# Layer norm's variance scaling on ScalarE, decays loaded ahead in two pieces, and a new order of work

## The chip, the cores and the metric

One core of a Trainium2 chip. The metric is the device time of one execution, in microseconds. The engines are named as in the profile: PE (TensorE, the matmuls), PEld (its weight loads), DVE (VectorE), ACT (ScalarE), POOL (GpSimd) and SP (SyncE, which here issues every transfer).

## What is computed

The reference is a chain of three layers on a batch of 4 sequences of 768 tokens, all in float32: a linear attention with decaying state (8 heads of 48), a gated layer with a spatial product over tokens, and a second gate with a convolution over 5 tokens.

```python
# attention, per batch and head, token by token
cur = einsum('bhd,bhe->bhde', u[None] * kt, vt)
y[:, :, t] = einsum('bhd,bhde->bhe', rt, state + cur)
state = wt[:, :, :, None] * state + einsum('bhd,bhe->bhde', kt, vt)
# gated layer: 384 -> 2 x 512 -> 384
u, v = split(gelu(x @ w_in))
v_n = (v - mean(v)) / sqrt(var(v) + 1e-06) * g_ln
gated = u * (einsum('ts,bsd->btd', w_sg, v_n) + b_sg[None, :, None])
x = x + gated @ w_out
# second gate
gate = sigmoid(causal_conv5(x, conv_w))
out = (gate * (x @ w_val)) @ w_out2
```

## The kernel before

**Attention.** The 768 tokens of a batch are cut into 3 segments of 256, the 8 heads into 4 pairs, which gives 48 units (batch, segment, pair), numbered in that order. Each unit loads one packet (`load_unit`, word "pk"): 128 rows of 773 columns, of which the first 261 are the decays, then 256 of k and 256 of r. Two scans along the decays on DVE give the products of decays after (F, `suffix`) and before (E, `prefix`) each token in chunks of 64; both read the decays alone. POOL or DVE multiplies r by E (L) and k by F (K). PE transposes K (t), forms scores (s), the states' growth (B) and the output (C). ACT copies out of PSUM (kx, gx, yc, ox), DVE masks the scores (mx), adds up the states (a), carries them to the next segment (z) and adds to the output (yx). U is ACT's start of a segment's state from the carried one. In the first batch only, ACT also forms the current token's term (ow), and PE runs filler matmuls on constants ("wm", "wps"). From the third batch on POOL forms that term (`bonus`).

**The other layers.** Per batch the output is transposed on PE (xT, with ACT and DVE splitting it into a high and a low part, xTo). Then come the layer's second half with its layer norm (hv, ln), the first half (u), the product over tokens (vs, vso, gate), the first output product (wo, woo), the convolution (cv), the value product (val, valo) and the last product (out), whose three tiles of 128 tokens ACT copies and SP sends off (outo). Every product is done in three passes of high and low parts. The weights come as float64 and are decoded by one ACT and four DVE instructions each (`to_f32`, word "dec"), then split ("spl"); "wl" are their loads. The token weights are loaded by "sg", v by "nat" and "sv", the constants by "ld". The wl loads share buffers: wl6 to wl8 overwrite the buffer of wl3 and wl4, which dec3 and dec4 read.

**Layer norm** (`hv`, lines 687 to 699), for each of 24 token tiles: ACT applies gelu and sums (line 691), centres (692), squares and sums (693); DVE scales the sum of squares to the variance with eps (line 695, 128x1); POOL raises it to the power -1/2 (696); ACT and DVE write the high and the low part (697, 698).

**The order of work.** Each step records its instructions under a word, such as "ln0" for the first layer norm, instead of issuing them. `SCHEDULE` (lines 55 to 193) lists the words; each mention issues the next part of the word: up to 16 instructions in a row on PE, 3 for some words, otherwise one (lines 956 to 969). An instruction that uses another engine starts a new part. So the list fixes the order on every engine and on SP's queue of transfers, while what waits for what follows from the tiles:

```python
            for _ in range(int(times or 1)):
                for f, a, k in parts[word].pop(0):
                    f(*a, **k)
```

In the profile all these instructions have line 969, the loop that issues them, so they are told apart by tile. Packets of the units have the tiles pk, room_l or room_w; F and E are the scans' outputs; st are states; s and rsw are ACT's copies; vg, vnt, sm and rstd belong to the layer norm; ot is the output tile, p and o are PSUM.

Of the kernel before, what the change touches and what calls it, by code (L numbers as in the profile page):

```python
# [70 lines left out]
yc8 a6 ox9 s8 spl4 ow26 mx11 B7 spl8 yx8 a6 C6 ow25 sg4 F9 gx23 K9 gx21 z6 U9 wm35 a7 gx22 yd5 ow24  # L71
wm35 mx12 wm36 U8 a7 wm36 E9 ow27 ox10 t9 ox11 kx13 kx12 q9 L9 ow31 B8 yx10 ow30 ln0 yx9 ow29 a7 ln0
yc10 s9 F10 ow28 C7 spl8 nat3 sv11 kx14 yc9 ln0 sg3 yx11 xT2 E10 pk12 wm37 ln1 xTo2 wm37 wl9 wm38
gx26 xTo2 hv2 ox12 gx25 K10 gx24 mx13 ln1 z7 a8 wm38 yd6 a8 hv2 ow34 q10 yc11 ow35 a8 yd7 ow33 hv2
F11 U10 L10 ow32 C8 ln2 mx14 B9 ln0 s10 pk13 E11 xT3 t10 q11 wm39 L11 ox14 gx27 wm39 wm40 yc12 gx28
a9 wm40 kx15 K11 yc13 xTo3 yx12 mx15 a9 gx29 s11 q12 kx16 ox13 a9 C9 ow38 ln2 F12 U11 ln2 B10 spl7
K12 ow37 t11 spl7 ow36 wm41 yx13 kx17 xTo3 hv3 gx30 gx32 a10 gx31 yd8 spl6 wm41 wm42 a10 q13 ox15
wm42 ow39 spl6 ow43 mx16 B11 yx14 ln2 mx17 a10 C10 ow40 E12 ow42 yc14 hv3 gx34 F13 L12 ow41 gx33
ox17 hv3 gx35 yx16 ox16 yc15 a11 ow47 yd9 pk14 yx15 yc16 ln1 ow45 s12 ln3 t12 K13 a11 dec6 a11 C11
E13 kx18 wm43 ow44 ln2 L13 ow46 wm43 spl12 nat4 yx17 xT4 mx19 sv12 yc17 F14 yd10 kx19 t13 xTo4 pk15  # L80
s13 spl13 B12 spl12 yd11 ln3 xT5 mx18 dec8 ln3 xTo4 hv4 kx20 spl13 gx36 xTo5 hv4 dec8 ln3 E14 hv4
gx37 dec8 L14 dec9 xTo5 hv5 gx38 a12 ln4 dec8 hv5 dec9 dec8 hv5 a12 wl11 dec9 u0 F15 ld2 ox18 ln5
o12 u0 ln4 ln3 u1 ln4 u1 mx20 z12 K14 ln4 B13 q14 s14 K15 C12 dec9 u1 ln4 sv14 wl13 vs0 E15 dec11
t14 dec9 vs0 dec11 spl15 vs0 wl10 q15 uo1 pk16 dec11 spl15 gx40 sv13 vs2 yc18 kx21 ln5 dec11 wl12
ln5 gx41 vs0 yx18 vs0 dec11 L15 dec10 gx39 u0 dec10 mx21 spl16 dec10 vs2 a13 uo0 dec10 spl16 spl14
vs1 dec10 a13 ox19 F16 ln5 vs1 o13 dec13 vs1 cw0 z13 q16 dec12 vs2 dec13 ln5 vs2 dec12 vs1 dec13 vs2
dec12 dec13 vs1 dec12 vs2 dec13 vs1 dec12 spl18 spl14 s15 spl17 wl15 B14 K16 C13 i0 E16 t15 spl17
# [956 lines left out]
```

## Time and profile before

| | |
|---|---|
| median of 3 runs | 474.2 us (473.36 to 474.63) |
| the profiled execution | 474.3 us, of which the span of its instructions is 472.5 us |
| mean granted clock of PE | 0.992 |
| busy: PE, PEld, DVE, ACT, POOL | 450.6, 406.3, 385.0, 266.9, 162.3 us |
| moved by DMA | 48.91 MB |
| sizes of the first loads | packet 386.5 KB, a piece of w_in 512.0, v 384.0, sv 96.0, ident 64.0, misc 38.5 KB |
| chain that ended last | PE 77%, DVE 9%, ACT 5% |

Times in rows are microseconds from the start of the span, unless marked ns. A busy time is the union of the engine's instructions. A bracket behind a row holds the engine's idle time ahead of the instruction and what ended it. The clock is the share of full speed that PE was granted.

### The profile page before, as it was taken

What the parts mean: (1) busy time and instruction counts of PE and PEld (TensorE: products, weight loads), DVE (VectorE), ACT (ScalarE), POOL (GpSimd) and SP (SyncE); (2) the same over time, 40 slices, a digit from 0 to 9 for tenths busy, and PEclk for the clock granted to TensorE, in tenths of its full rate; (3) what the DMA queues carried; (4) which work ended last, traced back from release to release, by engine and by line L of the source; (5) the groups of instructions that cost most, each with busy time, mean ns of one, the idle gap of its engine ahead of it and who ended that gap; (6) DMA issues with size and microseconds to landing.
All of it is one profiled execution on the core that took longest, in us unless ns stands there. A gap on an engine that the chain in (4) does not pass through costs nothing.

```text
span 472.5 us, 13805 instructions
## 1 busy us (share of the span) xinstructions
PE 450.6 (95%) x5556; PEld 406.3 (86%) x5556; DVE 385.0 (81%) x944; ACT 266.9 (56%) x786; POOL 162.3 (34%) x221
## 2 busy tenths in 40 slices
...
GB/s 278 354 261 167 1 163 111 187 154 114 130 50 116 157 185 68 60 74 152 125 67 135 171 92 85 51 85 135 54 39 147 10 2 1 50 2 0 1 1 100
DMA packets 27088, 48.91 MB, mean 103 GB/s; under 512 B 3088, under 2 KB 17168, under 8 KB 27024
## 3 DMA queue, kind: packets, MB, share of 16 engines
...
q8 instruction: 43, 0.70, 0.6%
q14 instruction: 21, 0.17, 0.1%
...
## 4 chain that ended last, share of the span: by engine, by line
PE 77%; DVE 9%; ACT 5%; issue 1%; DMA 1%; SPq 0%; ACTq 0%; DVEq 0%
PE vps L969 19%; PE p L969 13%; PE hv L969 10%; PE c L969 9%; PE ups L969 9%; PE o L969 8%; PE val L969 7%; PE a L969 2%; DVE cvp L969 1%; DVE st L969 1%; ACT st L969 1%; ACT vg L969 1%; DVE y L969 1%; DVE F L969 1%; DVE vps L969 1%
## 5 line engine op out<-in xcount | busy, mean ns | idle before, releaser
L969 PE MATMUL vps<-wsg,vnt 128*128 128x384 f32 x576 | 115.5, 339 | 1.4 <-DVE gt L969 0.7
L969 PEld LDWEIGHTS vps<-wsg,vnt 128*128 128x128 f32 x576 | 100.3, 188 | 3.0 <-ACT ut L969 1.6
L969 PE MATMUL ups<-x,win 128*128 128x384 f32 x288 | 61.4, 340 | 0.8 <-DVE gl L969 0.8
L969 ACT ACTIVATE st<-p,F 128x48 f32<-128x48 f32 x144 | 40.3, 304 | 38.0 <-PE p L969 36.7
L969 POOL TENSOR_TENSOR L<-pk,E 128x256 f32<-128x256 f32 x38 | 28.3, 744 | 94.7 <-PE p L969 32.9
L969 PE MATMUL c<-gl,late 128*128 128x384 f32 x288 | 59.9, 339 | 0.0
L969 PE MATMUL hv<-win,x 128*128 128x512 f32 x216 | 59.3, 405 | 0.3 <-ACT x L969 0.3
L969 DVE SCALAR_TENSOR_TENSOR cvp<-x,cw_col,cvp 128x384 f32<-128x384 f32 x84 | 50.6, 613 | 2.1 <-ACT cvp L969 1.6
L969 PEld LDWEIGHTS ups<-x,win 128*128 128x128 f32 x288 | 50.6, 188 | 1.7 <-DVE gl L969 1.1
L969 PEld LDWEIGHTS c<-gl,late 128*128 128x128 f32 x288 | 50.2, 188 | 1.0
L969 DVE SCALAR_TENSOR_TENSOR st<-st,F 128x48 f32<-128x48 f32 x128 | 39.3, 307 | 14.0 <-ACT st L969 13.0
L969 PE MATMUL o<-late,ml 128*128 128x384 f32 x216 | 46.9, 343 | 0.2
L969 PEld LDWEIGHTS hv<-win,x 128*128 128x128 f32 x216 | 38.7, 188 | 8.3 <-DVE x L969 0.9
L969 PE MATMUL val<-x2hl,late 128*128 128x384 f32 x216 | 43.6, 340 | 0.8 <-ACT ut L969 0.8
L969 POOL TENSOR_TENSOR x<-x 128x384 f32<-128x384 f32 x24 | 25.4, 1070 | 44.7 <-DVE cvp L969 43.0
L969 PEld LDWEIGHTS o<-late,ml 128*128 128x128 f32 x216 | 37.9, 188 | 2.8 <-DVE ml L969 1.4
L969 PEld LDWEIGHTS val<-x2hl,late 128*128 128x128 f32 x216 | 37.5, 188 | 1.9 <-ACT ut L969 1.1
L969 ACT ACTIVATE gl<-vps 128x384 fp32r<-128x384 f32 x29 | 14.3, 493 | 33.8 <-DVE vps L969 20.1
L969 POOL TENSOR_TENSOR y<-s,y 128x96 f32<-128x96 f32 x48 | 22.2, 469 | 32.2 <-DVE y L969 17.1
L969 DVE TENSOR_TENSOR_SCAN F<-pk,D1F 128x260 f32<-128x260 f32 x40 | 28.9, 722 | 4.5 <-DMA pk<-in_pk_dram 4.3
L969 POOL TENSOR_TENSOR rstd<-rstd,misc 128x1 f32<-128x1 f32 x24 | 15.6, 650 | 46.0 <-DVE rstd L969 32.3
L969 ACT ACTIVATE ut<-ups 128x384 f32<-128x384 f32 x32 | 15.7, 490 | 25.5 <-PE ups L969 20.6
(133 smaller groups left out, 944.5 us busy)
## 6 DMA issues: line engine op xcount, KB each, us to landing
pk<-in_pk_dram SPq DMA_DIRECT2D x40, 386.5 KB, 3.5
v<-in_v_dram SPq DMA_DIRECT2D x12, 384.0 KB, 4.9
out_dram<-ot SPq DMA_DIRECT2D x24, 192.0 KB, 1.9
rk<-in_rk_dram SPq DMA_DIRECT2D x12, 384.0 KB, 3.3
sv<-in_sv_dram SPq DMA_DIRECT2D x39, 96.0 KB, 3.0
bits<-in_w_in_dram SPq DMA_DIRECT2D x6, 512.0 KB, 7.4
room_l<-in_pk_dram SPq DMA_DIRECT2D x7, 386.5 KB, 6.7
bits<-in_w_o_dram SPq DMA_DIRECT2D x7, 384.0 KB, 4.2
```

Of the source, the lines that this page charges most:

```text
L969: f(*a, **k)
```

## The change

The variance's scaling and eps move from a DVE instruction to an ACT one (Identity with scale and a bias tile, which POOL fills at the start). The packets of units 0 and 1 are each loaded by two transfers, the decays first. Of the very last output tile ACT copies 208 columns and DVE 176. The words "rk" and "bon" are named by batch, and the list of words is written anew throughout. Its beginning, the part around the first layer norms and the last line stand here, then the rest of the diff.

```diff
@@ -53,144 +53,146 @@
 SCHEDULE = """
-ini0 pk0 zp0 wps0 pk1 pk2 ld0 wl0 ld1 wl1 nat0 F0 wl2 E0 sv0 q0 L0 F1 wl4 K0 pk3 E1 s0 dec0 sv3 wm4
-F2 L1 wl3 wm4 wm0 dec0 t0 K1 q1 nat1 kx0 dec1 t1 dec0 kx1 s1 E2 sv9 B0 dec1 wm1 gx1 L2 mx1 gx2 wm2
-mx0 dec1 wm9 dec2 K2 sv10 wm9 dec1 wm10 pk4 gx0 ox0 kx2 B1 dec0 dec4 sv1 wm10 dec2 wm3 a0 dec2 t2 a0
-C0 sv2 dec2 sg0 s2 dec1 wm5 ox1 yc0 kx3 wm6 ow2 dec4 gx4 wm7 F3 ow0 sg1 wm8 kx4 gx5 wm11 ow6 K3 z0
-wm12 mx2 dec3 wm13 dec0 pk5 gx3 wm15 wl5 ow3 dec4 ox2 pk7 ow7 q2 B2 ow1 dec2 spl1 sv4 wm14 a1 spl0
-dec3 wm15 wm16 a1 dec3 wm16 E3 q3 L3 mx3 yx0 yx1 wm21 dec4 t3 dec3 s3 C1 dec4 wm17 gx7 dec3 wm18
-spl10 wm19 F4 yc1 wm20 wl6 ox3 ow5 yd0 wm23 ow9 sv6 spl9 wm21 spl10 K4 wm22 pk6 wm22 spl2 z1 wl7 mx4
-E4 yc2 wl8 ow4 U4 sv5 kx5 spl9 L4 gx6 sv7 B3 yx2 pk10 dec5 a2 wm24 sv8 gx8 q4 ow10 s4 sg2 a2 ow8 C2
...
-C4 dec7 spl5 xTo1 hv1 ox7 kx9 U6 mx10 ow18 F7 hv0 spl3 ow20 sg5 gx17 ox8 gx15 ow23 z4 mx8 yc6 kx10
-a5 ow16 wm31 K7 ow22 mx9 wm31 yx6 gx16 wm32 q6 ln0 wm32 a5 hv1 dec6 a5 wm33 E7 hv1 F8 spl4 L7 wm33
-wm34 ln1 t7 q7 C5 E8 B6 s7 dec7 L8 wm34 gx18 z5 gx20 a6 ow21 K8 kx11 yx7 ln1 gx19 q8 yc7 U7 t8 yd4
...
-valo23*2 out69 out68 outo21 out67 outo21 out70 out71 outo22*2 outo23*2"""
+ini0 pk0 zp1 wps0 pk1 pk0 wl0 pk2 ld1 F0 pk1 wl2 E0 ld0 K0 nat0 F1 wl1 L0 dec0 wl4 E1 dec0 wl3 wm4
+q0 sv0 s0 dec0 F2 wm0 pk3 K1 wm4 wm1 dec0 t0 L1 t1 kx0 sv1 dec2 E2 pk4 kx1 s1 wm2 q1 wl5 L2 dec2 B0
+K2 wm3 gx1 mx1 ox0 mx0 gx0 pk5 dec2 dec1 wm9 dec0 wm5 ow0 wm9 gx2 wm6 q2 wm10 dec1 dec4 sv8 wm10 a0
+dec1 wm7 kx2 dec2 s2 B1 a0 dec3 sv4 dec1 wm8 sv2 wm11 dec2 t2 wm12 dec1 spl2 wm13 dec4 C0 spl0 dec3
+ow2 F3 kx4 gx5 ox1 ox2 K3 mx2 ow5 gx3 z0 dec3 yc1 kx3 wm15 gx4 E3 wm14 wm15 q3 B2 L3 mx4 yx0 wm16
+dec4 pk10 wm16 a1 sg0 dec3 s3 sv5 a1 C1 sv9 dec3 nat1 wm17 dec4 spl9 sv6 wm18 F4 t3 ow3 sg1 gx7 sv3
+ow1 K4 mx3 ox3 kx5 z1 yx1 yc0 spl9 ow9 zp0 wm21 gx6 ow4 wm19 a2 gx8 dec4 B3 ow6 dec5 a2 wl6 wm21 E4
+ow11 wm22 ow8 pk6 wm22 q4 spl10 L4 sv7 C2 mx5 ow7 sg2 z2 F5 yd0 s4 pk9 wm20 wl7 dec5 K5 t4 wm23 sv11
+kx6 yx4 ox4 wm24 yc3 E5 sv10 kx7 wm25 gx9 yc2 pk8 ox5 ow10 dec5 L5 U4 mx6 gx10 yx2 gx11 pk7 dec5
...
+mx8 hv0 kx10 xTo1 ox8 kx9 gx15 F7 hv1 spl3 spl4 sg5 U5 pk11 hv1 mx10 ow21 mx9 nat2 ow17 a5 U6 hv1 K7
+gx16 sg3 z4 ow23 a5 ow19 wm31 gx17 q6 wm31 ln1 a5 C5 E7 B6 F8 L7 wm32*2 dec7 ox7 t7 U8 K8 ow20 s7 z5
+yx6 yx7 gx19 dec7 yc6 ox9 ow22 wm33 gx18 E8 ow27 wm33 hv0 kx11 q7 yc7 gx20 a6 wm34 yd4 U7 a6 ln0
...
+out65 valo22 out66 valo23*2 out69 out68 outo21 out71 outo21 out67 out70 outo22*2 outo23*3"""
@@ -233,6 +235,7 @@
     cw_col = const.tile([128, KD, TAPS], F32, name="cw_col")
     win = const.tile([128, 2, KD, 2 * DV], F32R, name="win")
     D1F = const.tile([128, NW + 1], F32, name="D1F")
+    eps_col = const.tile([128, 1], F32, name="eps_col")
     u_bc = const.tile([128, DM], F32, name="u_bc")
 
 
@@ -368,12 +371,12 @@
 
     def load_rk(i):
         t = buf("rk", i, i // KS).rearrange("p (two f) -> p two f", two=2)
-        with step("rk"):
+        with step(f"rkb{i // KS}x"):
             sp.dma_start(out=t, in_=rk_[i // KS, i % KS * 128:(i % KS + 1) * 128, :, :])
 
     def bonus(b, i):
         s, j = divmod(i, NT)
-        with step("bon"):
+        with step(f"bonb{b}x"):
             t = buf("rk", b * KS + i, b)
             q = t[:, 0:DM]
             pool.tensor_tensor(out=q, in0=q, in1=t[:, DM:2 * DM], op=ALU.mult)
@@ -390,7 +393,8 @@
     def load_unit(n):
         b, s, p = units[n]
         with step("pk"):
-            sp.dma_start(out=buf("pk", n), in_=pk[b, p, s])
+            for x, y in ((0, OK_), (OK_, PK)) if n < 2 else ((0, PK),):
+                sp.dma_start(out=buf("pk", n)[:, x:y], in_=pk[b, p, s, :, x:y])
 
     def load_sv(n):
         b, s, p = units[n]
@@ -692,7 +696,7 @@
             act.activation(out=vg, in_=vg, func=AF.Identity, scale=-float(DV), bias=sm[:, 0:1])
             act.activation(out=hi, in_=vg, func=AF.Square, accum_out=sm[:, 1:2])
             rs = r2.tile([128, 1], F32, tag="rstd", name="rstd")
-            dve.tensor_scalar(out=rs, in0=sm[:, 1:2], scalar1=1.0 / DV, scalar2=EPS * DV * DV, op0=ALU.mult, op1=ALU.add)
+            act.activation(out=rs, in_=sm[:, 1:2], func=AF.Identity, scale=1.0 / DV, bias=eps_col)
             pool.tensor_tensor(out=rs, in0=rs, in1=mhalf, op=ALU.pow)
             act.activation(out=hi, in_=vg, func=AF.Copy, scale=rs)
             dve.scalar_tensor_tensor(out=vnt[b][:, 1, i, :], in0=vg, scalar=rs, in1=hi.bitcast(F32),
@@ -836,7 +840,10 @@
             for j in range(3):
                 with step("outo"):
                     t = rgt.tile([128, DM], F32, tag="t", name="ot")
-                    act.activation(out=t, in_=acc2[0][j], func=AF.Copy, scale=0.5)
+                    cut = 208 if (b, hf, j) == (B - 1, 1, 2) else DM
+                    act.activation(out=t[:, 0:cut], in_=acc2[0][j][:, 0:cut], func=AF.Copy, scale=0.5)
+                    if cut < DM:
+                        dve.tensor_scalar_mul(out=t[:, cut:DM], in0=acc2[0][j][:, cut:DM], scalar1=0.5)
                     t0 = hf * HALF + j * 128
                     sp.dma_start(out=out[b, t0:t0 + 128, :], in_=t)
 
@@ -883,6 +890,8 @@
     with step("ini"):
         dve.memset(D1F, 0.0)
         dve.memset(D1F[:, 0:NW + 1:W1], 1.0)
+    with step("zp"):
+        pool.memset(eps_col, EPS * DV * DV)
     for t in every("D1E"):
         with step("zp"):
             pool.memset(t, 0.0)
```

## Rows read from the trace of the kernel before

**Rows 1.** Busy time by stage: stretch, length, PE, PEld, DVE, ACT, POOL, clock, DMA, GB/s.

```profile
0.00:11.00 11.00, 7.66 (x61) 3.67 (x61) 5.70 (x13) 2.13 (x3) 4.09 (x9) 1.00 0.80 268
11.00:45.00 34.00, 27.54 (x559) 21.81 (x558) 33.72 (x92) 22.81 (x87) 15.03 (x17) 1.00 0.79 275
45.00:61.00 16.00, 13.34 (x286) 10.36 (x283) 11.60 (x35) 12.72 (x45) 8.89 (x14) 0.79 0.15 43
61.00:93.00 32.00, 30.49 (x523) 24.51 (x520) 29.81 (x88) 27.69 (x98) 14.96 (x20) 1.00 0.47 145
93.00:133.00 40.00, 36.19 (x476) 33.11 (x477) 39.52 (x104) 22.82 (x67) 17.21 (x23) 1.00 0.41 130
...
160.00:463.00 303.00, 303.00 (x3122) 283.93 (x3121) 237.75 (x546) 162.29 (x435) 93.22 (x125) 1.00 0.24 74
```

**Rows 2.** DVE in order of time: start, duration, what, idle time before.

```profile
4.11 0.70 DVE L969 TENSOR_TENSOR_SCAN F<-pk,D1F 128x260 f32<-128x260 f32 x1 [2.83 <-DMA pk<-in_pk_dram]
...
10.47 0.43 DVE L969 TENSOR_SCALAR spare<-spare 128x512 f32<-128x512 f32 x1 [1.26 <-ACT spare L969]
...
35.21 0.70 DVE L969 TENSOR_TENSOR_SCAN F<-room_l,D1F 128x260 f32<-128x260 f32 x1
...
42.88 0.84 DVE L969 TENSOR_TENSOR_SCAN F<-room_w,D1F 128x260 f32<-128x260 f32 x1
...
51.28 0.27 DVE L969 SCALAR_TENSOR_TENSOR st<-st,F 128x48 f32<-128x48 f32 x1 [1.87 <-ACT st L969]
...
51.64 0.14 DVE L969 TENSOR_SCALAR rstd<-sm 128x1 f32<-128x1 f32 x1
51.70 0.42 DVE L969 TENSOR_TENSOR pk<-pk 128x256 f32<-128x256 f32 x1
...
55.66 0.27 DVE L969 SCALAR_TENSOR_TENSOR st<-st,F 128x48 f32<-128x48 f32 x1 [0.88 <-ACT st L969]
```

**Rows 3.** DMA: KB each, us to landing; at 0-3, 43-47, 25-42 us, whole run.

```profile
bits<-in_w_in_dram SPq DMA_DIRECT2D x1, 512.0 KB, 7.2
...
spare<-in_w_sgT_dram SPq DMA_DIRECT2D x2, 192.0 KB, 2.5
...
DMA packets 2206, 4.28 MB, mean 252 GB/s; under 512 B 232, under 2 KB 1158, under 8 KB 2202
...
out_dram<-ot SPq DMA_DIRECT2D x24, 192.0 KB, 1.9
```

**Rows 4.** ACT in order of time.

```profile
9.76 0.68 ACT L969 ACTIVATE spare<-bits 128x512 f32<-128x512 f32 x1 [7.74 <-DMA bits<-in_w_in_dram]
...
45.07 1.28 ACT L969 ACT_TABLE_LOAD   x1
...
50.97 0.47 ACT L969 ACTIVATE st<-p,F 128x48 f32<-128x48 f32 x2
...
469.22 0.49 ACT L969 ACTIVATE ot<-o 128x384 f32<-128x384 f32 x1 [0.42 <-DMA out_dram<-ot]
```

**Rows 5.** PE in order of time.

```profile
12.31 0.45 PE L969 MATMUL p<-v,kn 64*64 64x48 f32 x16 [1.29 <-DMA v<-in_v_dram]
...
52.29 0.47 PE L969 MATMUL p<-ident,kh 128*128 128x128 f32 x1 [1.42 <-ACT s L969]
...
465.63 3.11 PE L969 MATMUL o<-late,ml 128*128 128x384 f32 x15
```

**Rows 6.** Busy time by stage, columns as in rows 1, five microseconds alone.

```profile
55.00:60.00 5.00, 4.97 (x98) 3.79 (x94) 3.20 (x11) 3.34 (x18) 3.64 (x6) 0.61 0.11 22
```

**Rows 7.** Groups of instructions, DVE and ACT: count, busy us, mean ns, idle before.

```profile
L969 DVE TENSOR_SCALAR rstd<-sm 128x1 f32<-128x1 f32 x24 | 3.4, 145 | 2.0 <-ACT vnt L969 1.8
...
L969 ACT ACTIVATE y<-v,rsw 128x48 f32<-128x48 f32 x48 | 14.9, 345 | 0.1
```

**Rows 8.** SP's issues of transfers in order of time.

```profile
25.88 0.33 SPq L969 DMA_DIRECT2D bits<-in_w_o_dram  x1
...
26.73 0.71 SPq L969 DMA_DIRECT2D room_l<-in_pk_dram  x1
```

More of the change, by code (lines that the diff above doesn't have):

```diff
@@ L71 @@
[L71 to L87, printed above, removed]
@@ L98 @@
-u6 yx22 o17 gate4 pk21 yd16 cv1 sv17 gate4 uo6 a17 gate4 cv2 a17 val0 cv1 kx25 U19 val0 a17 cv0 val0
-z17 cv0 cv2 val1 cv1 mx25 xT7 valo0 t19 s19 F20 valo0 B18 C17 cv2 valo0 out0 gx54 sv19 yc23 kx26 a18
-cv2 gx55 out1 gx56 U20 a18 vs5 E20 vs5 cv2 L20 vs5 yx23 cv2 a18 yd17 valo1 ox24 out2 o18 mx26 z18
-K20 valo1 C18 q20 s20 F21 pk22 B19 sv20 t20 valo1 vs5 gx57 E21 gx58 kx27 vs5 xTo7 a19 L21 mx27 out4
-yx24 out3 a19 gx59 K21 ox25 yc24 out5 a19 U21 o19 z19 xTo7 s21 yd18 C19 q21 F22 B20 pk23 sv21 t21
@@ new lines @@
+kx12 wm35 a7 wm36 K9 ox11 spl6 mx12 wm36 yx10 a7 yc9 ln0 B8 E9 ow24 gx23 ow28 t9 a7 ow29 L9 yx9 C7
+F10 ow30 ow31 ln0 ln1 s9 nat3 gx24 pk12 spl8 a8 ln1 yx11 xT2 ld2 yc10 E10 gx25 wm37 xTo2 wm37 wm38
+q9 ox12 L10 kx14 wm38 xTo2 yc11 hv2 ow33 q10 yd6 gx26 ln1 a8 hv2 K10 mx13 ln0 z7 a8 hv2 yd7 F11 spl7
+spl8 C8 ln2 mx14 s10 q12 t10 B9 E11 wm39 pk13 ln0 U9 L11 wm39 gx28 wm40 wl9 gx27 mx16 xT3 ow35 a9
+wl8 kx16 wm40 gx29 K11 kx15 a9 ow32 B10 ox14 yc12 ow39 q11 s11 ox13 ln2 a9 C9 xTo3 F12 ln2 ow34 t11
@@ new lines @@
+U10 mx15 spl7 xTo3 hv3 ln2 yx13 yx12 ow38 E12 hv3 yc14 gx30 gx31 a10 ow37 wm41 dec6 gx32 wm41 wm42
+U11 a10 ow36 wm42 a10 yc13 ox15 K12 kx17 C10 yd8 ow40 F13 ow42 B11 L12 ow41 ow43 hv3 yc16 ln1 ox17
+gx34 yc15 spl6 ox16 pk14 ow45 gx35 yx14 gx33 ln3 mx17 yx15 a11 yd9 yx16 t12 a11 K13 s12 q13 wm43 a11
+ow47 E13 ow46 C11 ln3 ln2 ow44 L13 wm43 kx18 spl13 yx17 xT4 kx19 mx18 yc17 F14 yd10 spl12 pk15 B12
+xTo4 nat4 s13 spl12 yd11 sv12 t13 xTo4 dec8 hv4 ln3 mx19 gx37 spl13 ox18 gx36 xT5 kx20 hv4 E14 xTo5
@@ new lines @@
+vs5 uo4 K19 ox23 gate4 u6 a17 pk21 mx25 cv0 u6 q20 gate4 u6 a17 yx22 val0 uo6 a17 cv1 val0 woo2 vs5
+z17 val0 cv2 F20 yc22 U19 s19 yd16 cv2 B18 o17 valo0 t19 cv2 valo0 C17 K20 U20 valo0 out0 gx54 cv1
+cv2 yc23 val1 gx56 gx55 a18 cv2 ox24 val1 o18 mx26 out1 cv2 a18 kx26 E20 xT7 val1 a18 xTo7 L20 yx23
+out2 z18 valo1 t20 pk22 F21 valo1 s20 B19 valo1 C18 E21 out3 gx57 sv20 gx58 a19 kx27 sv19 vs5 a19
+gx59 K21 yc24 ox25 out5 U21 a19 o19 mx27 out4 z19 L21 yx24 q21 B20 yd18 xTo7 s21 yd17 C19 F22 t21
```

216 lines of the change are left out of this document (112 added, 104 removed).

## The prediction

> **What bounds the kernel now.** I read first the table of busy time by stage [rows 1]. From 160 to 463 us the matmul engine (PE) is never idle: 303.00 of 303.00 us, while VectorE (DVE) works 237.75 us and ScalarE (ACT) 162.29 us. No change can make that stretch shorter, only open gaps in it. So a gain has to come from the 160 us before it, or from the last ten. Before 133 us the engine with the least idle time is DVE: its busy times in the first five stages are 5.70, 33.72, 11.60, 29.81 and 39.52 us, together 120.35 of 133 us. Its idle time is 5.30 us in the first 11 us, 0.28 in the next 34, 4.40 from 45 to 61 us, 2.19 up to 93 and 0.48 up to 133: 12.65 us. PE runs filler matmuls ("wm") in that time and still has gaps. I take the first 133 us to be bound by DVE's list of work plus DVE's idle time, and the rest by PE. So the sum is made of what DVE's idle time loses or gains, and of DVE instructions that leave its list ahead of that point.
>
> Second I read what DVE waits for in the two stages with idle time: at the start the first packet and then, by way of ACT, the first piece of the input weights; from 45 to 61 us the state copies of ACT [rows 2].
>
> **The head: transfers in pieces, and their new order.** Before, DVE's first scan starts at 4.11 us after 2.83 us idle, when all 386.5 KB of the packet are there [rows 2]. Now it needs 261 of 773 columns, 130.5 KB. A transfer of 192 KB on a quiet queue takes 2.5 us from issue to landing [rows 3]; I take 2.4 us, so the scan starts at 3.1 us, 1.0 us sooner (ends: 1.2 us, and nothing if the pieces issued behind it compete fully). But the next wait takes some of this back. DVE's list is now F0, E0, F1, E1 and then the decode step dec0 of the weights, ahead of q0 and F2, which stood ahead of it before. The four scans with their reciprocals are about 3.4 us, so DVE is free at 6.5 us. ACT can start dec0 when the first piece of w_in has landed; that was at 9.76 us [rows 4], with 1710 KB queued up to its end. Now 130.5 + 130.5 + 256 + 512 = 1029 KB are, and it is issued half a microsecond sooner. In proportion to the bytes still queued that gives 6.6 us; with the 7.2 us that it took from issue to landing [rows 3] it is 9.3 us. I take 7.2 us, near the first, since the shorter queue is what differs. With 0.7 us of ACT the decode starts on DVE at 7.9 us, after 1.4 us idle. DVE's idle time in the head is then 0.9 + 1.8 + 1.5 = 4.2 us against 5.30, a lead of 1.1 us (1.7 and -1.0 at the two ends). The two added issues on SP are covered: the queue is what limits, and v, for which PE waits 1.29 us at 12.31 us [rows 5], has 2670 KB up to its end in either order, so it lands as before. The second decode, dec1, has its weights 3182 KB deep instead of 2286 and may cost DVE up to 0.7 us. I book **-0.8 us** for the head.
>
> **45 to 61 us: the new order on ACT.** ACT loads a table for 1.28 us at 45.07 us, then runs the three long layer norm activations of one token tile, a split of 0.5 us, and the three of the next tile; only at 50.97 us come the state copies [rows 4]. So a tile's three take some 2.1 us. For the copies DVE waits 1.87 us and, 4 us later, another 0.88 us [rows 2]. PE has a gap of 1.42 us there, behind ACT [rows 5], and after it the granted clock falls to 0.61 of full speed, a mix of 1.2 and 2.4 GHz [rows 6]. In the new order one tile's three activations (ln1) go first, then ox7, U8, ow20, gx19, yc6, ox9, ow22, gx18, ow27, kx11, yc7, gx20, U7, and the other tile's three (ln0) only behind them. The block ahead of the state copies is shorter by 2.1 us and the 0.5 us split, but seven short activations of some 0.24 us stand ahead of gx18, which DVE's a6 needs. Net the copies come some 0.9 us sooner, and so does yc7, the one that PE waited for. The second block then falls into the 3.3 us in which ACT is idle in this stage [rows 1]. Ends: nothing, if the wait turns up one unit later, and 3.5 us, if the clock stays up and both waits go. I take **-1.5 us**, between, since the waits are shortened and not removed.
>
> **The variance scaling.** 24 VectorE instructions of 128x1 go, of 145 ns each [rows 7]; the next instruction starts 0.06 us behind one of them [rows 2], so six in the DVE-bound stretch are worth 0.4 to 0.9 us, and I take **-0.4 us**, since the next start is what counts on a full engine. The other 18 lie where PE is full and save nothing. On ACT 24 instructions of 128x1 with pointer operands come in. The trace has none; the nearest are the 128x48 products with a pointer scale, 345 ns long [rows 7]. I take 0.2 us, since a part of each lies under the next (ends 0 and 0.3). ACT is idle 4.3 of the 32 us from 61 to 93 us [rows 1], and six at 0.2 us are 1.2 us; a third of it on the path is **+0.4 us** (0 to 1.8). GpSimd's power now waits for ACT instead of DVE; behind it on GpSimd stand splits and products of later units, and who waits for its result is ACT, much later. The Trainium skill's page "ScalarE: Activation LUTs", section "Rules for kernel authors", speaks against this edit: adds and multiplications belong on VectorE. Its section "What ACT_TABLE_LOAD costs" gives 280 ns for an activation with a pointer bias, 93 ns of it overlapped, an estimate of 0.19 us each. By that rule the edit loses, as in the third rival.
>
> **The rest of the order.** DVE's list ahead of the first output product (word out0) has 339 instructions before and 335 after: six scalings gone, K20 and q20 added. No work is moved out of the bound stretch, and I book 0; what it may open on SP is the second rival. The renamed words add nothing. The memset of eps goes to GpSimd, which is idle 6.9 of the first 11 us [rows 1], and costs nothing; were it late, the first activation with it would wait, at about 55 us.
>
> **The tail.** The last tile's copy is 0.49 us on ACT, from 469.22 us, after 0.42 us of waiting for the transfer that frees its buffer [rows 4]. With 208 columns on ACT and 176 on DVE it takes some 0.33 us. But the matmul group that now comes last is the middle tile's: its copy can start only after PE's end at 468.74 us [rows 5], half a microsecond later than before, ahead of the last tile's first part on ACT. The last part is done at 469.55 to 469.7 us instead of 469.71, and two transfers of 192 KB, 1.9 us each [rows 3], leave back to back. I book **+0.1 us** (-0.2 to +0.5).
>
> **Sum.** -0.8 - 1.5 - 0.4 + 0.4 + 0.1 = -2.2 us against the profiled execution of 474.3 us (span 472.5 and 1.8 us around it). The median of the runs is 474.2, so the forecast is **472.0 us**. A measurement of this kernel can tell about 0.3% from no change, 1.4 us.
>
> **The rivals.** One, no difference that can be told: the lead of the head is lost in the wait for the first weights, and the wait for ACT at 51 us comes back one unit later. The scaling's two terms cancel, and half a microsecond is left: 473.7 us. For it: the two waits of DVE stand 4 us apart. Against: nothing takes the removed block's place on ACT.
>
> Two, slower, by the queue of SP. The load wl6 must wait for the last decode of the buffer that it overwrites. Before, it is issued at 25.88 us and pk6 at 26.73 us [rows 8], for a scan at 35.21 us; pk7 was issued before wl6, for a scan at 42.88 us [rows 2]. In the new order the last of those decodes is dec4 instead of dec3, two microseconds further down DVE's list, and pk7 stands behind wl6, pk6, sv7, sg2, pk9, wl7, two sv and pk8, 2.8 MB in all. At the 252 GB/s of that stretch [rows 3] these are 11 us after some 26.5 us: pk7 lands at 37.5 us, 4 us ahead of its scan at some 41.8 us. The mechanism decides when the queue is more than 4 us later than I think; 8 us later, it takes back all 2.2 us and 2.0 more: 476.2 us.
>
> Three, slower, by ACT: from 61 to 93 us it has the least room after DVE. If each moved scaling costs 0.3 us there and ACT ends last, six are 1.8 us instead of 0.4; with no gain of the order that is -0.4 + 1.8 + 0.1: 475.7 us. It decides if ACT's idle time there goes under 2 us.
>
> **The numbers.** The forecast's case has 0.56, the first rival 0.27, the second 0.10, the third 0.07. All ends of the terms would reach from 468 to 477; with no more than 2 in 10 outside, the range is 468.6 to 475.4 us: the low end has most of the 3.5 us of the second stage with the head's 1.7, the high end leaves out the two slower cases' own values. Faster by over 0.3% 0.56, within it 0.27, slower 0.17.
>
> **What would show it.** DVE's first scan at 3.1 us, and its wait for dec0 ending at 7.9 us; waits of DVE for state copies from 45 to 61 us under 1 us each, and less time at the lower clock there; DVE's idle time up to 133 us near 10.5 us; ACT's idle time from 61 to 93 us shorter by about 1 us; PE full from about 131 us on. Wrong it is if PE has gaps after 160 us, if a scan waits for its packet between 30 and 45 us, or if DVE's idle time only moves.

## The result, and the profile after

The changed kernel takes 477.83 us (median of 20 runs, 475.1 to 481.5), the kernel before 474.31 us (20 runs, 472.0 to 477.3). The ratio is 1.0068, with a 95% interval of 1.0047 to 1.0089: 0.7% slower. The forecast was 472.0 us, with 475.4 us as the upper end.

The profiled execution took 476.6 us, with a span of 474.4 us (before: 474.3 and 472.5). The page's first part, after:

```profile
PE 452.3 (95%) x5556; PEld 406.4 (86%) x5556; DVE 384.9 (81%) x921; ACT 271.7 (57%) x810; POOL 162.7 (34%) x222
```

Busy time by stage, after, with the columns of [rows 1]; the two lines behind "..." cut one stage finer:

```profile
0.00:11.00 11.00, 8.42 (x48) 3.94 (x48) 6.39 (x15) 2.70 (x4) 4.22 (x9) 1.00 0.83 273
11.00:45.00 34.00, 29.85 (x571) 22.44 (x571) 33.25 (x90) 22.51 (x86) 14.89 (x19) 0.95 0.73 247
45.00:61.00 16.00, 12.94 (x300) 10.45 (x297) 14.42 (x41) 15.28 (x56) 9.75 (x15) 1.00 0.41 128
61.00:93.00 32.00, 29.26 (x508) 23.37 (x507) 30.03 (x79) 26.46 (x94) 13.47 (x18) 0.95 0.47 143
93.00:133.00 40.00, 35.64 (x472) 31.94 (x471) 39.48 (x100) 22.25 (x65) 16.80 (x21) 1.00 0.42 124
...
160.00:463.00 303.00, 302.79 (x3120) 283.92 (x3119) 233.34 (x528) 165.68 (x458) 96.95 (x129) 1.00 0.24 74
...
70.00:74.00 4.00, 2.27 (x70) 1.65 (x68) 3.97 (x10) 3.55 (x17) 2.88 (x4) 1.00 0.37 103
74.00:78.00 4.00, 3.89 (x57) 2.43 (x56) 2.96 (x10) 2.49 (x10) 1.40 (x2) 0.57 0.05 5
```

Two things stand in these lines. DVE's idle time up to 133 us is 4.61 + 0.75 + 1.58 + 1.97 + 0.52 = 9.43 us, against 12.65 in [rows 1]: it fell by 3.2 us, more than the 2.2 us that the forecast lived on. But DVE was busy for 123.57 us there instead of 120.35, though six scalings had left its list. It worked 3.2 us more and got no further. The second thing is PE at 70 to 78 us: idle for 1.7 us, then at a granted clock of 0.57, ahead of a dense stretch.

What DVE did longer shows in its own timeline, after, set against [rows 2] and [rows 5]:

```profile
3.02 0.70 DVE L978 TENSOR_TENSOR_SCAN F<-pk,D1F 128x260 f32<-128x260 f32 x1 [1.75 <-DMA pk<-in_pk_dram]
...
8.04 0.43 DVE L978 TENSOR_SCALAR spare<-spare 128x512 f32<-128x512 f32 x1 [1.69 <-ACT spare L978]
...
48.44 0.42 DVE L978 TENSOR_TENSOR y<-p,y 128x96 f32<-128x96 f32 x2 [1.01 <-ACT rsw L978]
...
60.24 0.28 DVE L978 TENSOR_TENSOR L<-p,misc 128x128 f32<-128x128 f32 x1
60.44 0.19 DVE L978 TENSOR_TENSOR cy<-p,st 128x48 f32<-128x48 f32 x1
60.55 1.09 DVE L978 SCALAR_TENSOR_TENSOR st<-st,F 128x48 f32<-128x48 f32 x1
...
70.51 1.18 DVE L978 TENSOR_TENSOR_SCAN F<-pk,D1F 128x260 f32<-128x260 f32 x1
71.72 0.18 DVE L978 RECIPROCAL D1E<-F 128x4 f32<-128x4 f32 x1
71.81 1.23 DVE L978 SCALAR_TENSOR_TENSOR vnt<-vg,rstd,vnt 128x512 fp32r<-128x512 f32 x1
72.97 0.34 DVE L978 TENSOR_TENSOR y<-p,y 128x192 f32<-128x192 f32 x1
...
75.71 0.72 DVE L978 SCALAR_TENSOR_TENSOR vnt<-vg,rstd,vnt 128x512 fp32r<-128x512 f32 x1
```

A state update, 0.27 us in [rows 2], lasts 1.09 us, a scan, 0.70 us there, 1.18 us, and ln1's last part, 0.72 us for the next tile at 75.71 us, 1.23 us. No wait is booked: the time is inside the instruction. GpSimd's timeline, after, shows what ran beside them:

```profile
59.38 0.88 POOL L978 TENSOR_TENSOR room_w<-room_l,F 128x256 f32<-128x256 f32 x1
60.21 0.38 POOL L978 TENSOR_TENSOR y<-s,y 128x96 f32<-128x96 f32 x1
60.56 1.02 POOL L978 TENSOR_TENSOR wsg<-spare,wsg 128x384 fp32r<-128x384 f32 x1
...
70.26 0.86 POOL L978 TENSOR_TENSOR L<-pk,E 128x256 f32<-128x256 f32 x1
71.09 1.41 POOL L978 TENSOR_TENSOR wsg<-spare,wsg 128x384 fp32r<-128x384 f32 x1
```

The update at 60.55 us ends 0.06 us after the subtraction for the token weights (words "spl", tile wsg) that began with it. The scan and ln1's part lie on L and the next subtraction. PE then waits for the y that follow them (PE's timeline, after):

```profile
71.17 0.96 PE L978 MATMUL hv<-win,x 128*128 128x512 f32 x3
73.86 0.74 PE L978 MATMUL p<-ident,kh 128*128 128x128 f32 x2 [1.73 <-DVE y L978]
```

To count this over whole traces I take the 322 DVE instructions that start before 133 us in the kernel before and are the same in all kernels, and for each of them what it lasts beyond the shortest that it has in any of the 20 traces. (Two instructions overlap a little, so each counts from the end of the one before it.) I call the sum DVE's **excess**. It is 7.8 us before and 11.9 us after: 4.1 us more, against 3.2 us of idle time saved. The last of the 322 starts at 135.0 us instead of 132.9. From 45 to 80 us alone it is 2.2 and 5.3 us. (The expectations below quote 7.1 to 7.3 and 11.4 to 11.7: the same count over fewer traces.)

### The profile page after: what moved, and what is told of

It reads as the page before. It is cut to its first block, busy times and chain, and to the rows that moved or that the text cites. A ratio compares the mean times of both kernels' runs of the same rounds, so it can differ in the third digit from the quotient of the medians.

```text
span 474.4 us, 13802 instructions
## 1 busy us (share of the span) xinstructions
PE 452.3 (95%) x5556; PEld 406.4 (86%) x5556; DVE 384.9 (81%) x921; ACT 271.7 (57%) x810; POOL 162.7 (34%) x222
## 4 chain that ended last, share of the span: by engine, by line
PE 77%; DVE 10%; ACT 5%; DMA 3%; issue 2%; SPq 1%; POOL 1%; ACTq 0%; DVEq 0%; POOLq 0%
PE vps L978 18%; PE p L978 13%; PE c L978 10%; PE ups L978 9%; PE hv L978 9%; PE val L978 8%; PE o L978 8%; DVE spare L978 2%; PE a L978 2%; ACT vg L978 1%; DMA pk<-in_pk_dram 1%; DVE st L978 1%; DMA v<-in_v_dram 1%; PE wps L978 1%; ACT st L978 1%
## 5 line engine op out<-in xcount | busy, mean ns | idle before, releaser
L978 PE MATMUL ups<-x,win 128*128 128x384 f32 x288 | 59.9, 339 | 0.3 <-DVE gl L978 0.2
L978 ACT ACTIVATE st<-p,F 128x48 f32<-128x48 f32 x144 | 39.2, 303 | 36.3 <-PE p L978 35.4
L978 DVE SCALAR_TENSOR_TENSOR st<-st,F 128x48 f32<-128x48 f32 x128 | 40.4, 316 | 8.5 <-ACT st L978 6.6
L978 DVE SCALAR_TENSOR_TENSOR vps<-vps,misc,b_bc 128x384 f32<-128x384 f32 x29 | 18.0, 622 | 18.4 <-PE vps L978 18.3
L978 PEld LDWEIGHTS <-D1F 128*128 128x128 bf16 x196 | 19.1, 105 | 14.6 <-issue 7.3
L978 POOL TENSOR_TENSOR y<-s,y 128x96 f32<-128x96 f32 x48 | 20.9, 438 | 29.3 <-ACT s L978 15.8
```

## The experiments

Every run was measured in five rounds beside the kernel before. "Clock" is the median over its runs of the mean granted clock; for the kernel before it was 0.991 or 0.992 each time. Single runs go with it: the changed kernel's took 475.1 us at 0.996 and 481.5 us at 0.982. Differences in the text are those of the ratios, times 474 us.

A run takes longer the lower its mean clock, so part of a difference can be the clock's. To take it out I fit the spans of the runs in the table, and of the kernel before beside them, with one level for each kernel and one slope for all: 0.26 us of span for 0.001 of mean clock. The difference of two levels is what I call the difference **at equal clock**; its 95% uncertainty is 0.4 to 0.7 us. For the changed kernel it is 2.0 us against the kernel before, of the 3.2 us that the ratio gives. Some 0.7 us are the clock's, and 0.3 us lie outside the span of the instructions.

| run | median us | ratio to before, 95% interval | clock | excess us |
|---|---|---|---|---|
| changed kernel | 477.8 | 1.0068 (1.0047 to 1.0089) | 0.988 | 11.9 |
| tail_back | 477.1 | 1.0053 (1.0032 to 1.0075) | 0.988 | 11.9 |
| scale_back | 476.2 | 1.0045 (1.0017 to 1.0072) | 0.993 | 12.4 |
| pieces_back | 478.5 | 1.0083 (1.0050 to 1.0116) | 0.988 | 11.4 |
| order_alone | 478.0 | 1.0074 (1.0050 to 1.0098) | 0.987 | 11.7 |
| edits_old_order | 478.5 | 1.0083 (1.0051 to 1.0115) | 0.989 | 10.4 |
| scale_old | 476.2 | 1.0049 (1.0026 to 1.0072) | 0.992 | 10.2 |
| scale_old_early | 477.4 | 1.0062 (1.0033 to 1.0092) | 0.993 | 10.8 |
| pieces_old | 477.0 | 1.0047 (1.0024 to 1.0069) | 0.988 | 7.8 |
| gap_fix | 475.9 | 1.0021 (1.0000 to 1.0042) | 0.994 | 11.0 |
| repairs | 477.2 | 1.0051 (1.0027 to 1.0075) | 0.993 | 12.2 |
| best | 476.6 | 1.0039 (1.0016 to 1.0063) | 0.992 | 12.2 |
| head67 | 474.3 | 0.9993 (0.9971 to 1.0015) | 0.996 | 12.1 |
| old_min | 475.2 | 1.0006 (0.9979 to 1.0033) | 0.992 | 9.9 |
| old_min2 | 475.0 | 1.0010 (0.9984 to 1.0037) | 0.992 | 7.9 |
| nospl_new | 472.9 | 0.9954 (0.9928 to 0.9981) | 0.995 | 10.1 |
| nospl_old | 473.0 | 0.9948 (0.9925 to 0.9972) | 0.994 | 7.0 |
| zeros3_new | 473.4 | 0.9971 (0.9944 to 0.9997) | 0.994 | 9.5 |
| zeros3_old | 474.2 | 0.9993 (0.9969 to 1.0017) | 0.993 | 8.4 |

### The parts of the change, undone and alone

**tail_back** (of the new list, the end alone):

```diff
-                    cut = 208 if (b, hf, j) == (B - 1, 1, 2) else DM
+                    cut = DM
-... outo21 out71 outo21 out67 out70 outo22*2 outo23*3
+... outo21 out67 outo21 out70 out71 outo22*2 outo23*2
```

> The changed kernel with the last output tile copied by ScalarE alone and the last three output products in the order of before. Theory A (most of the loss is made by the new order between 60 and 130 us, and the tail adds a smaller piece): from PE's last matmul to the end of the span 3.75 us as before instead of 4.47, so 0.7 us comes back and some 2.8 of the 3.5 us stay: 477.1 against 474.3 us, ratio 1.006. Rival B (the tail is the loss): within 0.5 us of the kernel before. Rival C (the two engines copy the tile side by side and the tail is no loss): no change against the changed kernel, ratio 1.0075.

1.0053: 0.7 us less than the changed kernel, as theory A had it, though the two intervals overlap. The changed kernel's trace shows why the tail lost (all engines, last microseconds):

```profile
468.71 1.22 PE L978 MATMUL o<-late,ml 128*128 128x384 f32 x6
...
470.02 0.73 ACT L978 ACTIVATE ot<-o 128x384 f32<-128x384 f32 x2 [1.63 <-PE o L978]
...
470.77 0.34 DVE L978 TENSOR_SCALAR ot<-o 128x176 f32<-128x176 f32 x1 [3.46 <-ACT ot L978]
```

DVE's 176 columns wait for ACT's 208: the copies run one behind the other, and both behind the middle tile's. From PE's end at 469.93 us to the end of the span it is 4.5 us; before it was 3.8 us [rows 5].

**scale_back:**

```diff
-            act.activation(out=rs, in_=sm[:, 1:2], func=AF.Identity, scale=1.0 / DV, bias=eps_col)
+            dve.tensor_scalar(out=rs, in0=sm[:, 1:2], scalar1=1.0 / DV, scalar2=EPS * DV * DV, op0=ALU.mult, op1=ALU.add)
```

> The changed kernel with the 24 scalings of the variance back on VectorE, at the same places of the list. Theory A (the new order loses, the scaling is worth nothing either way): the changed kernel's time within 0.7 us, ratio to the kernel before 1.005 to 1.009. Rival D (ScalarE with the scalings ends last from 61 to 93 us, 0.3 us each for six of them): 1.4 to 1.8 us come back, ratio 1.003 to 1.004. If instead VectorE's list is the bound and the scalings' 0.06 to 0.145 us each count there, it is 0.4 to 0.9 us longer than the changed kernel.

1.0045: 1.1 us less, between the two theories and not certain by itself (the intervals overlap). ACT's group for it lasts 292 ns each, twice DVE's 145 in [rows 7]:

```profile
L978 ACT ACTIVATE rstd<-sm,eps_col 128x1 f32<-128x1 f32 x24 | 7.0, 292 | 0.2
```

**order_alone** takes back all three edits and leaves the new list; **edits_old_order** has the three edits in the old list; **pieces_back** takes back the pieces alone (`for x, y in ((0, PK),):`).

> The new order of work alone: scaling on VectorE, packets in one piece each, the last tile copied by ScalarE alone, the last three output products in the new order. Theory A: the whole loss less the tail's 0.2 us for the two parts, plus the head's lead that the pieces gave: 1 us for the first scan, so 3 to 4.5 us slower than before, ratio 1.006 to 1.0095. Rivals B and D (the edits lose, not the order): within 0.9 us of the kernel before, ratio under 1.002.

> The kernel before with the three edits (scaling on ScalarE, the two packets in two pieces, the last tile on two engines) in its old order of work. Theory A: what loses is the order, so this stands within 0.9 us of the kernel before, -0.9 to +0.5 us (pieces let the first scan start 1 us sooner, the last tile's two parts run one behind the other and cost 0.2 us): ratio 0.998 to 1.001. Rival D or B (the edits lose): over 1.5 us slower, ratio above 1.003.

> The changed kernel with the first two packets in one piece each; the list is otherwise the new one. Theory L (in the new order the pieces bring the first scan 1 us forward, and the old order could not use them): 0.3 to 1.8 us slower than the changed kernel, ratio to the kernel before 1.0075 to 1.0105. Rival M (as in the old order, where the pieces alone made it 2.2 us longer, they cost here too): 1 to 2.5 us faster than the changed kernel, ratio 1.0015 to 1.0045.

The order alone loses 3.5 us (1.0074), as expected. That the edits in the old order lose just as much (1.0083) was not expected by theory A: both halves lose by themselves, and together they lose no more. So the parts don't add. Taking the pieces out of the new order gave 1.0083, 0.7 us longer than the changed kernel; theory L's sign, but within the uncertainty.

**scale_old**, **pieces_old**: one edit each in the old list, beside the renamed words and GpSimd's fill of the bias tile. The old list issues the two pieces of a packet one behind the other, the new one both units' decays first. **scale_old_early**: as scale_old, with 15 of the 24 scalings moved in the list directly behind their squares.

> The kernel before with the scaling on ScalarE alone, in the old order. Theory I (in the old list ln4's scaling stands behind ln5's three activations, so GpSimd's power comes late, ln4's last activation waits 0.80 us at 87.04 us and the two ut behind it make PE late): most of the 4.3 us that the three edits lost in the old order, 2 to 4 us, ratio 1.004 to 1.0085. Rival J (it is the pieces or the tail): under 1 us, ratio under 1.002.

> The kernel before with the first two packets in two pieces alone, in the old order. Theory I: the first scan starts 1 us sooner, v and the weights land when they did, so 0 to 0.8 us faster, ratio 0.998 to 1.0005. Rival J (the two added transfers delay the identity, v and the weights behind them, for which PE waits at 10 and 12.4 us): 0.5 to 2 us slower, ratio 1.001 to 1.004, with PE's gap at t0 over 1 us as with all three edits (1.25 us against 0.51).

> As scale_old (the kernel before with the scaling on ScalarE), with the scaling of 15 of the 24 token tiles, ln4 among them, directly behind its own square instead of where VectorE's had stood. Theory I (on ScalarE the scaling queued behind the next tile's three activations, so GpSimd's power was late and ln4's last activation waited for it): that wait of 0.80 us is under 0.2 us, PE's gaps behind ut at 93 and 97 us (0.90 and 0.55 us) shrink to the 0.65 us of before, and 0.6 to 1.5 us of scale_old's 2.3 come back: ratio 1.0015 to 1.0035. Rival K (ScalarE's time for 24 more instructions is what costs, wherever they stand): as scale_old, 1.004 to 1.006.

The scaling alone costs the old order 2.3 us. Theory I's wait is in the trace (ACT's timeline, scale_old): the scaling is issued behind the next tile's activations, so GpSimd's power comes late.

```profile
88.74 0.28 ACT L981 ACTIVATE rstd<-sm,eps_col 128x1 f32<-128x1 f32 x1
89.82 0.72 ACT L981 ACTIVATE vnt<-vg,rstd 128x512 fp32r<-128x512 f32 x1 [0.80 <-POOL rstd L981]
```

But with the scaling early, PE's waits behind ut at 93 and 97 us were gone and the time was not better (1.0062). So that wait was not the loss. What both kernels have in common is an excess of 10.2 and 10.8 us instead of 7.8: moving small instructions between engines was enough to make others meet. The pieces alone leave the excess at 7.8 and still cost 2.2 us. Their runs had a lower clock (0.988), and at equal clock 1.0 us is left. Rival J's sign, a longer wait of PE at t0 for the identity, is there (PE's timeline; it was 0.51 us before):

```profile
10.53 0.66 PE L981 MATMUL p<-ident,kh 128*128 128x128 f32 x4 [1.31 <-DMA ident<-in_ident_dram]
```

But scale_old, without the pieces, has 0.99 us there, and the trace of pieces_old shows no loss of position behind 45 us. Where the clock fell in the other runs isn't in a trace. That cause stays open.

### The waits of PE

**gap_fix** (list): ln1's fifth entry goes from ahead of ox17 to behind t12. **repairs**: besides, z15 behind the second a15, z16 behind the third a16, the fourth vs4 behind s18. **best**: repairs, with the edits of tail_back and scale_back.

```diff
-... hv3 yc16 ln1 ox17 ... mx17 yx15 a11 yd9 yx16 t12 a11 K13
+... hv3 yc16 ox17 ... mx17 yx15 a11 yd9 yx16 t12 ln1 a11 K13
```

> The changed kernel with one VectorE instruction moved: ln1's last part (128x512, 1.23 us in the changed kernel's trace at 71.81 us) behind yx15 and yx16, where the old order has it. Theory E (the new order makes PE wait 1.73 us for yx14 and yx15 at 73.86 us, behind a scan and ln1's last part that both ran long beside GpSimd; after that wait the granted clock is 0.50 for 3.4 to 10 us ahead of the dense stretch from 80 us): the gap falls under 0.7 us, no stretch at half clock follows it, and the time is 1.2 to 3 us shorter than the changed kernel's 477.8: 475 to 476.6, ratio to the kernel before 1.002 to 1.005. Rival F (the wait only moves to the next step of PE, or is not what lowers the clock): within 0.7 us of the changed kernel, ratio 1.0055 to 1.0085.

> The changed kernel with four entries of its list moved: ln1's last part behind yx15 and yx16 (as in gap_fix), z15 directly behind the second a15, z16 directly behind the third a16, and the fourth vs4 behind s18. Theory E (the loss is made of new waits of PE between 72 and 128 us, each of which may also be followed by a stretch at half clock): the waits of 1.64 us at C15 and 1.37 us at vs4 fall under 0.8 us each, and 1 to 3 us come off gap_fix's 475.9: 473 to 475, ratio to the kernel before 0.997 to 1.001. Rival F (a wait of PE that goes comes back at the next step): as gap_fix, ratio 1.001 to 1.004.

> The list of repairs, and besides the scaling on VectorE, the last tile copied by ScalarE alone and the last three output products in the order of before; the first two packets stay in two pieces. Sum of the parts as measured so far, each with an uncertainty of about 1 us: after 477.8, less 1.9 (gap_fix), 1 to 3 (the other two waits), 1.1 to 1.6 (scale_back), 0.7 (tail_back): 471 to 473, ratio 0.993 to 0.998, faster than both kernels. Rival F, or parts that don't add: 474 to 475.5, ratio 0.9995 to 1.003.

In gap_fix the wait at t12 halves (PE's timeline):

```profile
74.68 0.68 PE L981 MATMUL p<-ident,kh 128*128 128x128 f32 x2 [0.84 <-DVE y L981]
```

Theory E wanted less than 0.7 us. The kernel is 2.2 us shorter than the changed one, as theory E expected, with intervals that don't overlap; at equal clock 0.6 us of this are left, no more than the uncertainty. And repairs and best hold the same move and are at 1.0051 and 1.0039, slower than either theory had it. In repairs' trace the wait at vs4 is under 0.6 us, but the one at C15 is 1.78 us, where it was 1.64. What the traces agree on is the clock. In five kernels of the new order PE waits 1.6 us or more at t12, and in four of them a stretch at half clock follows between 74 and 85 us; in the five with 1.0 us or less none does. In the old order all nine traces have such a stretch between 52 and 61 us. A further one, between 11 and 20 us, stands in five traces of either order and in head67's, so one trace doesn't tell a kernel's clock. Over the path the moved waits gave little: rival F, mostly. **best** beats neither what it was summed to (0.993 to 0.998) nor the kernel before.

**head67**: the new list's first 510 entries, then the rest in the old order, scaling on DVE, old tail.

> The new order up to its 510th entry (67 us of the changed kernel's trace), then whatever is left in the order of before; scaling on VectorE, the first two packets in two pieces, the tail as before. Theory E: PE's lead of 1.2 us at 65 to 70 us, that the new order had and gave back from 72 us on, is kept to the end, and the stretch at half clock is the old one or none: 473.0 us, ratio 0.9975 (0.995 to 0.9995). Rival G (the lead is only work brought forward, and the old order waits for the same things there): within 0.7 us of the kernel before. Rival H (the two orders do not fit together at the seam): slower by over 1 us.

0.9993: no difference, rival G. The lead of the head is not kept: the trace's excess is 12.1 us, with 3.7 us from 93 to 133 us, where the kernel before has 2.5. Its clock was the highest of the table; at equal clock it is 0.9 us longer than the kernel before.

### The wait for ScalarE at 51 us

**old_min** was meant to move ln1's three long activations behind yc7 in the old list and nothing else. As built, they came to stand between kx11 and gx19, still ahead of yc7. **old_min2** puts them behind yc7:

```diff
-... wm33 wm34 ln1 t7 q7 ... kx11 yx7 ln1 gx19 q8 yc7 U7 t8 ... F9 gx23
+... wm33 wm34 t7 q7 ... kx11 yx7 gx19 q8 yc7 ln1 U7 t8 ... F9 ln1 gx23
```

> The kernel before with two entries of its list moved: ln1's three long activations behind yc7 instead of ahead of gx18, and ln1's scaling behind F9. It is the step on which the forecast for 45 to 61 us stood, without the rest of the new order. Theory R (VectorE's wait of 1.87 us and PE's of 1.42 us at 51 to 52 us go, the stretch at half clock that followed them in the old order goes with them, and nothing else is disturbed): 1.2 to 2.5 us faster, ratio 0.9945 to 0.9975. Rival S (the wait comes back one unit later, or VectorE's instructions stretch by as much): within 0.7 us, ratio 0.9985 to 1.0015.

> The kernel before with ln1's three long activations really behind yc7 (in old_min they came to stand between kx11 and gx19, still ahead of yc7) and ln1's scaling behind F9, nothing else changed. Theory R (the old order's wait for ScalarE at 51 to 52 us was worth what was booked): VectorE's wait for gx19 (1.74 us in old_min) and PE's for yc7 (2.05 us) go under 0.6 us, VectorE's idle time from 45 to 61 us falls from 4.4 to under 3 us, and it is 1 to 2.5 us faster, ratio 0.9945 to 0.998. Rival S (VectorE's instructions stretch by as much or the wait comes back at the next unit): idle time from 45 to 61 us over 3.5 us or an excess over 9 us, and a ratio of 0.9985 to 1.0025.

Rival S in both, 1.0006 and 1.0010. DVE's timeline of old_min2, with its stage from 45 to 61 us below:

```profile
49.17 0.74 DVE L972 SCALAR_TENSOR_TENSOR st<-st,F 128x48 f32<-128x48 f32 x1 [0.39 <-ACT st L972]
...
52.87 0.42 DVE L972 TENSOR_TENSOR L<-p,misc 128x256 f32<-128x256 f32 x1 [2.28 <-ACT rsw L972]
...
45.00:61.00 16.00, 12.10 (x280) 9.06 (x279) 11.28 (x33) 12.38 (x44) 8.86 (x13) 0.79 0.18 55
```

The wait of 1.87 us [rows 2] is 0.39 us, and the next unit's waits 2.28 us for what now stands behind the block. DVE's idle time in the stage is 4.7 us, where it was 4.4.

### What GpSimd reads

**nospl_new** is tail_back, **nospl_old** the kernel before, with this edit; it leaves out the low part of the token weights. In **zeros3_new** and **zeros3_old** the zeros are written three times, so that GpSimd is busy as long as with the subtraction.

```diff
-            (e or pool).tensor_tensor(out=lo, in0=t, in1=hi.bitcast(F32), op=ALU.subtract)
+            if e is None or e is pool:
+                pool.memset(lo.bitcast(F32), 0.0)
+            else:
+                e.tensor_tensor(out=lo, in0=t, in1=hi.bitcast(F32), op=ALU.subtract)
```

> tail_back (the changed kernel with the old tail) in which GpSimd writes zeros into the low part of the token weights instead of subtracting, so that it reads nothing there; that leaves out the low part of the token weights. Theory P (in the first 133 us VectorE's instructions last 4.1 us longer in the new order, 11.4 to 11.7 us over their shortest against 7.1 to 7.3 in the old, because other pairs of VectorE and GpSimd instructions meet; some 3 us of that lie beside these subtractions): VectorE's excess falls by 2 to 3 us to 8.5 to 9.5, and the time by 1.5 to 3 us against tail_back's 477.1: ratio to the kernel before 0.999 to 1.002. Rival Q (the long instructions are not the path, or others take their place): excess or time as in tail_back, ratio 1.004 to 1.007.

> The kernel before with the same zeros instead of GpSimd's subtraction (the low part of the token weights is left out). Theory P: in the old order only 0.4 to 1.0 us of VectorE's excess lie beside the subtractions, so 0 to 1 us faster, ratio 0.998 to 1.0005, and the distance between the two orders shrinks from 2.5 us to 1 or less. Rival Q: unchanged, ratio 0.9985 to 1.0015, and the distance stays.

> As nospl_new, with the zeros written three times: 3 x 0.41 us, so that GpSimd is busy about as long as with the subtraction (1.17 us in the changed kernel) and still reads nothing there. Theory P (what lengthens VectorE's instructions is that GpSimd reads two operands beside them, not that it is busy): VectorE's excess within 0.7 us of nospl_new's 9.4, time within 0.9 us of nospl_new's, ratio to the kernel before 0.9935 to 0.998. Rival T (what helped in nospl_new was that GpSimd was done 0.76 us sooner twelve times, so that PE's waits for the token weights went): most of the 4.6 us between tail_back and nospl_new are lost again, ratio 1.001 to 1.005, with a wait of over 1 us at vs4.

> As nospl_old, with the zeros written three times: GpSimd as busy as with the subtraction (1.12 us in the kernel before) without reading. Theory P: within 0.9 us of nospl_old, ratio 0.993 to 0.997, and VectorE's excess at 6.3 us within 0.7. Rival T: back at the time of the kernel before, ratio 0.998 to 1.001.

Twelve subtractions stand behind this. Without them the 2.5 us between the two orders are gone: tail_back falls by 4.7 us to 0.9954, the kernel before by 2.5 us to 0.9948. That was more than theory P gave, so GpSimd's shorter time had a share. The zeros written three times tell them apart. The old order is back at 0.9993 (rival T there: it was GpSimd's length that had helped), while the new order stays at 0.9971, 3.9 us under tail_back with intervals far apart (theory P). GpSimd's group in zeros3_new, and DVE there at the two places shown above:

```profile
L985 POOL MEMSET wsg<- 128x384 f32 x36 | 15.3, 431 | 1.4
...
60.62 0.25 DVE L985 SCALAR_TENSOR_TENSOR st<-st,F 128x48 f32<-128x48 f32 x1
...
69.74 0.89 DVE L985 TENSOR_TENSOR_SCAN F<-pk,D1F 128x260 f32<-128x260 f32 x1
...
70.75 0.89 DVE L985 SCALAR_TENSOR_TENSOR vnt<-vg,rstd,vnt 128x512 fp32r<-128x512 f32 x1
```

The twelve subtractions took 13.9 us of GpSimd after, the zeros 15.3 us: as busy, but not reading. The state update is back at 0.25 us; the scan and ln1's part come down to 0.89 us. The excess falls from 11.9 to 9.5 us. And here the new order is the shorter one, 0.9971 against 0.9993, about 1 us, though the intervals overlap.

The zeros differ in one more way, which no run separates: they need no input, while the subtractions wait for ScalarE's high part, in the changed kernel for 5.3 us of GpSimd's time:

```profile
L978 POOL TENSOR_TENSOR wsg<-spare,wsg 128x384 fp32r<-128x384 f32 x12 | 13.9, 1167 | 5.4 <-ACT wsg L978 5.3
```

Two things speak against it as the cause. In zeros3_old the old order is rid of 6.9 us of the same waits and is no faster. And up to 160 us PE's waits for wsg fall only from 1.4 us in tail_back to 1.1 us in zeros3_new.

## Why the prediction was wrong

**What bounds the kernel** held: PE is full from 160 us (302.79 of 303.00 us), and DVE has the least idle time before. But the sum was made of idle time and of instructions that leave the list, as if an instruction's duration belonged to it.

**The head** came as forecast: the first scan at 3.02 us (3.1), the decode on DVE at 8.04 us (7.9) after 1.69 us (1.4), idle time 4.61 us (4.2). pieces_back has the sign for it, no more.

**45 to 61 us:** the waits shrank as described. The longest for ACT is 1.01 us, the stage's idle time 1.58 instead of 4.40 us, its clock 1.00 instead of 0.79, and ACT is busy for 15.28 us instead of 12.72, since the second block of long activations falls into its free time. Booked were 1.5 us; the idle time gave 2.8. Made alone, the move is worth nothing (old_min2): the first rival's mechanism, the wait one unit later. It needs the list around it.

**The scaling:** 0.29 us on ACT, the upper end of the estimate, not 0.2. The third rival's place was wrong, since ACT's idle time from 61 to 93 us grew to 5.54 us; its sign was right, with 1.1 us in the new order (uncertain) and 2.3 us in the old (certain). There the wait behind it was not the price, as scale_old_early shows. On the rule of the Trainium skill that spoke against the edit ("ScalarE: Activation LUTs", "Rules for kernel authors"), the runs agree with its sign.

**The rest of the order, booked at 0 with no range, is the step that failed.** The number of instructions ahead of the bound's end was right, their length was not: the new order lets other instructions of DVE and GpSimd meet, and the same 322 last 4.1 us longer. That takes back the 3.2 us of idle time and the lead. By the matmuls done, PE's own useful work was 1.2 us ahead of the kernel before at 60 us, level at 75 us, where PE's wait at t12 and the half clock lie, and 1.6 us behind at 130 us. zeros3_new shows it: take the reading away at twelve places, and 3.9 us come back. Of these, 2.4 us show as excess in the traces and 2.1 us (0.7 either way) are left at equal clock, where zeros3_new is level with the kernel before; the rest goes with a higher clock, 0.994 instead of 0.988, and what raised it is not settled. The profile's page could have told: "a" (st<-st,F) had a mean of 307 ns before, while the rows at 51.28 and 55.66 us [rows 2] have 0.27 us.

The Trainium skill's page "SBUF — State Buffer", section "Who interferes with whom", states the rule: a DVE instruction with two SBUF inputs contends with a GpSimd instruction that reads SBUF, not with one that only writes. The traces agree. In the 16 traces with the subtraction, DVE instructions with an operand in PSUM (mx, yx, z, xTo, vso) met GpSimd 1949 times and none was over 0.2 us longer than its shortest; of 1821 meetings of those that read SBUF twice (a, K, q and the scans), 400 were, and of 2723 of these that met no GpSimd instruction none. Which meetings cost follows from how much of GpSimd's instruction was left when DVE's began: with 0.3 us or more, 339 of 494 were lengthened, otherwise 61 of 1327. The convolution's steps (cv), which add into PSUM (cvp), were not lengthened in any of 512 meetings. In the gate the same operation occurs both ways: with its tile in PSUM (vps) none of 412 meetings lengthened it, with its tile in SBUF (gt) 13 of 33 did.

**The tail** was mis-sized: +0.7 us in the trace instead of +0.1, since the two copies don't run side by side. At equal clock, though, tail_back's span is no shorter than the changed kernel's, so what it costs in time is uncertain.

**The rivals:** SP's queue did not decide. wl6 was issued at 27.74 us, a microsecond later than thought; pk7 landed at 39.2 us, and its scan started at 42.45 us without a wait. No rival held the mechanism that did decide, and the range ended 2.4 us short, because a wholly new order had been given one value instead of two bounds.

Of the 0.7%, what is shown is that the stretched DVE instructions outweigh the idle time saved: 4.1 less 3.2 us, with the tail's 0.7, make 1.6 of the 1.9 us by which the two traces' spans differ, a sum and not an experiment. The tail (0.7), the scaling (1.1) and the half clock behind t12 each have a sign but no certain size, and they don't add: best, with all three undone, is still at 1.0039. Nor is the excess a price by itself: head67 has 12.1 us of it and takes no longer, pieces_old has no more than before and does.
